# A 64-byte gap moves behind w_gate's even chunks: attention and SwiGLU in one kernel on Trainium2

## The chip, the cores and the metric

The kernel runs on one core of one Trainium2 chip (trn2). The metric is the device time of one execution in microseconds (us); for three runs of the kernel before it was 1176.67 us in the median, 1175.26 to 1177.6. The engines of the core are named as in the profile: PE is TensorE (matmuls), PEld its weight loads, DVE is VectorE, ACT is ScalarE, POOL is GpSimd, SP is SyncE, whose queue issues most of the transfers. SBUF is the memory on the chip that the engines read, 128 partitions; an address here is a byte offset in a partition. PSUM is the memory into which TensorE writes.

## The reference

Block-causal attention of 8 batches, 8 heads, 576 tokens and head size 64, and behind it a SwiGLU feed-forward over the 4608 tokens, all in float32:

```python
scores = scale * np.matmul(q, k.transpose(0, 1, 3, 2))
scores = np.where(mask, scores, -1000000000.0)   # blocks of 64
...
attn = np.exp(scores)
attn = attn / (np.sum(attn, axis=-1, keepdims=True) + 1e-09)
x = np.matmul(attn, v)                            # as [4608, 512]
...
g = x @ w_gate                                    # [512, 1536]
silu = g * (1.0 / (1.0 + np.exp(-g)))
val = x @ w_val                                   # [512, 1536]
return (silu * val @ w_out).astype(np.float32)    # [1536, 512]
```

## The kernel before, in words

The 4608 tokens are cut into 18 tiles of 256. For each tile the feed-forward goes through the 1536 columns of w_gate and w_val in 12 chunks of 128, two chunks (an even one and the odd one behind it) to a stage: six stages to a tile, 108 in all. To keep float32 accuracy with the faster float32r matmul, each operand is split into a high and a low part, and a product is three matmuls: high by high, high by low, low by high. They are the lines 1105, 1106 and 1107 of the function `up`. In them the weights are the stationary operand (`lhsT`, 128 by 128, loaded anew for each matmul), and the tokens, the tiles `xhl`, are the moving one (128 by 256).

A stage computes, in this order, the even chunk of w_gate (array g_even in the profile), its odd chunk (g_odd), and the even and the odd chunk of w_val (both in v_all). The contraction runs over 512 rows, four pieces of 128, so each chunk takes 4 x 3 = 12 matmuls: 12 with g_even, 12 with g_odd, 24 with v_all, 48 to a stage. Then VectorE and ScalarE make silu(g) times val and split it into high and low parts (tiles `hhl`), and the down stage multiplies these with chunks of w_out (tiles `wo`) in the lines 1197 to 1199. There `hhl` is the stationary operand and `wo` the moving one, 128 by 512; the result goes to the PSUM tiles po or at. The down stage of one pair of chunks stands behind the up stage of a later one, so that TensorE alternates between the two kinds.

The attention of later batches is put between these stages: scores in line 569 (line 442 for the first batches, 653 for one of them), products with v in line 782. A planner written in the kernel (`in_order`) sorts all steps of all engines by ranks and by costs that are constants in the code; it doesn't look at addresses. From the fifth tile on (FINE = 4) the steps of an up stage are mostly kept together in the order above. In the first four tiles they are cut into pieces of three matmuls, and pieces of several stages and of attention come in mixed orders. The first two tiles run while the attention of the first two batches is still being made.

The weights come into the chip once. A transfer brings a raw chunk into a `wo` tile, ScalarE casts its high part into its place (line 983) and VectorE subtracts to get the low part (line 986). Those places are the six tiles at the head of the list of constants, each with the index 0 for the high and 1 for the low part. For some chunks of w_out, places in these arrays that are not yet taken serve as a temporary store (`AWAY`, line 915), from which they are written to memory (line 1005) and read by a few early down stages.

The tiles of the list lie behind one another in SBUF in the order of the list. Ahead of the weights stand `ident` (512 bytes to a partition), `ones` (256) and two single columns, and g_odd begins 64 bytes past a multiple of 128. A g_odd or g_even tile has 4 x 768 x 4 = 12288 bytes, a v_all tile 24576, both multiples of 128; so g_odd and v_all begin 64 bytes past a multiple of 128. Behind v_all stands a tile of 16 float32 numbers, 64 bytes, that nothing reads or writes (line 205). Behind it g_even begins at a multiple of 128, and so do the tiles of `xhl`, `wo` and `hhl` that follow.

Of the kernel before, what the change touches and what calls it, by code (L numbers as in the profile page):

```python
# [8 lines left out]
F32R = mybir.dt.float32r  # L9
# [9 lines left out]
def kernel(  # L19
# [75 lines left out]
    const = ctx.enter_context(tc.tile_pool(name="const", bufs=1))  # L95
# [106 lines left out]
    half_w, whole_w = [P, NDC, DFF // 2], [P, NDC, DFF]  # L202
    g_odd = [const.tile(half_w, F32R, name=f"g_odd{x}") for x in range(2)]
    v_all = [const.tile(whole_w, F32R, name=f"v_all{x}") for x in range(2)]
    const.tile([P, 16], F32, name="gap")
    g_even = [const.tile(half_w, F32R, name=f"g_even{x}") for x in range(2)]

    def w_at(which, x, i):

# [1246 lines left out]
```

## Time and profile before

| | |
|---|---|
| median of 3 runs | 1176.67 us (1175.26 to 1177.6) |
| the profiled execution | 1178.6 us |
| its span, from the first to the last instruction | 1176.7 us |
| mean granted TensorE clock | 0.991 |
| busy: PE, DVE, ACT, POOL | 1149.6, 746.6, 625.0, 322.1 us |
| moved by DMA | 197.41 MB |

The profile is one execution, taken by the hardware profiler. A busy time adds up the time in which an engine had an instruction at work. Matmuls are pipelined: one lasts some 280 ns from its start to its end, but the next starts after some 115 ns. What a matmul costs a busy TensorE is therefore the interval from its start to the start of the next one, and that is read from the timeline, not from the mean length. The timeline gives a start in us, a length in us, the engine, the line of the kernel, the operation, what it writes and reads by the names of the tiles, and the shape. A matmul is listed at the start of its streaming; the load of its weights is a row of PEld.

The rows of groups give a line, an engine, an operation and a shape, how often it occurs, the busy us and the mean ns of one, and the idle time of the engine ahead of it.

### The profile page before, as it was taken

To read this page: it belongs to the slowest core of one execution; us is meant where nothing else is said; L and a number is where in the kernel's file an instruction comes from. 1 tells how busy PE (TensorE), PEld (TensorE's weight loads), DVE (VectorE), ACT (ScalarE), POOL (GpSimd) and SP (SyncE) were. 2 spreads that over 40 slices of the span, in tenths; PEclk is the share of its full clock that TensorE was granted. 3 is DMA by queue.
4 is the path that set the end of the run, shared out by engine and by line. 5 is a ranking of instruction groups with operands and counts; after the bars stand their busy time and mean duration, and the time that the engine had idled before them with its cause. 6 is when DMAs were issued, how large, how long until landed. Compare 5 with 4: busy or idle time off the path is not lost.

```text
span 1176.7 us, 21979 instructions
## 1 busy us (share of the span) xinstructions
PE 1149.6 (98%) x8578; PEld 1029.6 (88%) x8578; DVE 746.6 (63%) x1230; ACT 625.0 (53%) x1114; POOL 322.1 (27%) x139
## 2 busy tenths in 40 slices
PE   6889999999999999999999999999999999999998
PEld 5567878888899998989899998989989898999997
DVE  5798889677678574768567674856648565423222
ACT  5788877646383655637374564637355463212111
POOL 3212100144523333422414332342424233000000
PEclk8899999999999999999999999999999999999999
DMA  7666858756574646755376544745556434654442
GB/s 202 168 169 189 208 178 259 190 175 175 162 180 134 172 143 172 210 176 129 132 201 199 146 150 134 216 140 163 157 161 192 166 108 148 199 160 133 146 166 103
DMA packets 266984, 197.41 MB, mean 168 GB/s; under 512 B 195264, under 2 KB 231376, under 8 KB 266880
## 3 DMA queue, kind: packets, MB, share of 16 engines
q1 hardware_dynamic: 264304, 195.29, 56.8%
q8 instruction: 67, 1.10, 0.4%
q10 hardware_dynamic: 2576, 0.72, 0.3%
q14 instruction: 37, 0.30, 0.1%
HBM read 171.57 MB, written 24.38 MB: 167 GB/s over the span
## 4 chain that ended last, share of the span: by engine, by line
PE 90%; DVE 3%; ACT 3%; DMA 2%; issue 1%; SPq 0%; POOL 0%; ACTq 0%; POOLq 0%; DVEq 0%
PE gv L1105 17%; PE gv L1107 16%; PE gv L1106 16%; PE po L1197 8%; PE po L1198 7%; PE po L1199 7%; PE at L782 7%; PE at L569 5%; PE at L653 1%; PE at L1197 1%; PE at L442 1%; PE at L1198 1%; PE at L1199 1%; DVE mx L710 1%; DMA qk<-in_k_dram 1%
## 5 line engine op out<-in xcount | busy, mean ns | idle before, releaser
L714 POOL PARTITION_ALL_REDUCE mx<-mx x80 | 141.0, 1811 | 441.7 <-DVE mx L710 131.6
L833 POOL PARTITION_ALL_REDUCE mx<-mx x48 | 178.5, 3766 | 229.1 <-DVE mx L710 210.0
L1105 PE MATMUL gv<-xhl,v_all 128*128 128x256 f32 x864 | 241.0, 279 | 0.0
L1107 PE MATMUL gv<-xhl,v_all 128*128 128x256 f32 x864 | 239.2, 277 | 0.0
L1106 PE MATMUL gv<-xhl,v_all 128*128 128x256 f32 x864 | 239.0, 277 | 0.0
L1142 DVE SCALAR_TENSOR_TENSOR t<-t,gv 128x512 f32<-128x512 f32 x108 | 73.8, 684 | 146.6 <-ACT t L1139 146.0
L1105 PEld LDWEIGHTS gv<-xhl,v_all 128*128 128x128 f32 x864 | 162.1, 188 | 3.4 <-issue 2.1
L1106 PEld LDWEIGHTS gv<-xhl,v_all 128*128 128x128 f32 x864 | 162.3, 188 | 0.8
L1155 DVE TENSOR_TENSOR hhl<-t,hhl 128x512 fp32r<-128x512 f32 x108 | 91.4, 847 | 112.3 <-ACT hhl L1152 109.0
L1107 PEld LDWEIGHTS gv<-xhl,v_all 128*128 128x128 f32 x864 | 162.2, 188 | 0.1
L1152 ACT CAST hhl<-t 128x512 fp32r<-128x512 f32 x108 | 67.3, 623 | 156.2 <-PE po L1198 114.4
L1197 PE MATMUL po<-wo,hhl 128*128 128x512 f32 x372 | 148.3, 399 | 0.7 <-ACT ob L1224 0.7
L1198 PE MATMUL po<-wo,hhl 128*128 128x512 f32 x372 | 145.6, 391 | 0.0
L1199 PE MATMUL po<-wo,hhl 128*128 128x512 f32 x372 | 145.3, 390 | 0.0
L738 DVE TENSOR_TENSOR sc<-sc,mx 128x640 f32<-128x640 f32 (+6 forms) x168 | 123.4, 774 | 20.4 <-POOL mx L714 20.4
L1139 ACT ACTIVATE t<-gv 128x512 f32<-128x512 f32 x108 | 64.6, 598 | 119.6 <-PE gv L1107 116.9
L1105 PE MATMUL gv<-xhl,g_even 128*128 128x256 f32 x432 | 124.2, 288 | 0.2 <-DVE t L1142 0.2
L742 ACT ACTIVATE sc<-sc 128x1024 f32<-128x1024 f32 (+3 forms) x104 | 105.8, 1030 | 32.5 <-DVE sc L738 31.4
L1106 PE MATMUL gv<-xhl,g_even 128*128 128x256 f32 x432 | 122.5, 283 | 0.0
L1107 PE MATMUL gv<-xhl,g_even 128*128 128x256 f32 x432 | 122.3, 283 | 0.0
L1105 PE MATMUL gv<-xhl,g_odd 128*128 128x256 f32 x432 | 120.4, 279 | 0.0
L1107 PE MATMUL gv<-xhl,g_odd 128*128 128x256 f32 x432 | 119.5, 277 | 0.4 <-DVE g_odd L986 0.4
(175 smaller groups left out, 2398.8 us busy)
## 6 DMA issues: line engine op xcount, KB each, us to landing
wo<-wo_d SPq DMA_DIRECT2D x200, 512.0 KB
out_dram<-ob SPq DMA_DIRECT2D x35, 256.0 KB
v<-in_v_dram SPq DMA_DIRECT2D x64, 128.0 KB
xt<-x_d SPq DMA_DIRECT2D x64, 128.0 KB
rt<-r_d SPq DMA_DIRECT2D x128, 64.0 KB
qk<-in_q_dram SPq DMA_DIRECT2D x112, 72.0 KB
qk<-in_k_dram SPq DMA_DIRECT2D x104, 72.0 KB
x_d<-xu SPq DMA_DIRECT2D x24, 288.0 KB
```

What stands on the lines that cost most here:

```text
L714: nc.gpsimd.partition_all_reduce(m, m, channels=P, reduce_op=bass_isa.ReduceOp.max)
L738: nc.vector.tensor_tensor(piece(c), scores_of(c), m, ALU.subtract)
L742: nc.scalar.activation(x, x, AF.Exp)
L782: nc.tensor.matmul(ps[0][own(x), 1 - i if sums else i, q0 - s0 : s1 - s0], lhsT=ones if sums else vt[0][:, 2 * lane + c, own(x)], rhs=sc[0 ...
L833: nc.gpsimd.partition_all_reduce(m, m, channels=P, reduce_op=bass_isa.ReduceOp.add)
L1105: nc.tensor.matmul(o, lhsT=hi[:, d], rhs=xhi[:, 0:w], start=first, stop=False)
L1106: nc.tensor.matmul(o, lhsT=hi[:, d], rhs=xlo[:, 0:w], start=False, stop=False)
L1107: nc.tensor.matmul(o, lhsT=lo[:, d], rhs=xhi[:, 0:w], start=False, stop=last)
L1155: nc.vector.tensor_tensor(hh[1][:, 0:n], t[0][:, 0:n], hh[0][:, 0:n].bitcast(F32), ALU.subtract)
L1197: nc.tensor.matmul(po, lhsT=hi, rhs=whi, start=i + y == 0, stop=False)
L1198: nc.tensor.matmul(po, lhsT=hi, rhs=wlo, start=False, stop=False)
L1199: nc.tensor.matmul(po, lhsT=lo, rhs=whi, start=False, stop=i + y == NFC - 1)
```

## The change

The unused tile of 64 bytes moves in the list from ahead of the g_even tiles to behind them. The two g_even tiles begin 64 bytes lower, 64 bytes past a multiple of 128 as g_odd and v_all do. What stands behind the gap in the list keeps its place. No instruction and no order is touched.

```diff
     half_w, whole_w = [P, NDC, DFF // 2], [P, NDC, DFF]
     g_odd = [const.tile(half_w, F32R, name=f"g_odd{x}") for x in range(2)]
     v_all = [const.tile(whole_w, F32R, name=f"v_all{x}") for x in range(2)]
+    g_even = [const.tile(half_w, F32R, name=f"g_even{x}") for x in range(2)]
     const.tile([P, 16], F32, name="gap")
-    g_even = [const.tile(half_w, F32R, name=f"g_even{x}") for x in range(2)]
```

## The prediction

> **What bounds the kernel now.** I read four views of the profile in this order: the page, the busy time by stretches together with the waits of TensorE, the groups of instructions by form, and the timeline of TensorE.
>
> From the page, the busy row of TensorE and the shares of the chain that ended last:
>
> ```profile
> PE 1149.6 (98%) x8578; PEld 1029.6 (88%) x8578; DVE 746.6 (63%) x1230; ACT 625.0 (53%) x1114; POOL 322.1 (27%) x139
> ...
> PE 90%; DVE 3%; ACT 3%; DMA 2%; issue 1%; SPq 0%; POOL 0%; ACTq 0%; POOLq 0%; DVEq 0%
> ```
>
> From the busy time by stretches (start and end, length, then busy us of PE, PEld, DVE, ACT and POOL), one row; then everything that TensorE waited for from 300 us to the end:
>
> ```profile
> 400.00:600.00 200.00, 200.00 (x1492) 183.45 (x1491) 130.70 (x206) 108.88 (x194) 70.33 (x24) 1.00 0.56 162
> ```
>
> ```profile
> PE po L1197 <- ACT ob L1224: 0.3, 1, 0.3
> PE gv L1105 <- DVE t L1142: 0.2, 1, 0.2
> ```
>
> TensorE is never idle between 400 and 600 us, at a granted clock of 1.00, and from 300 us on it waits 0.5 us in all. So from there on the time is the sum of the intervals between starts of matmuls: a nanosecond more or less on each comes out at the end one for one. A busy time cannot show these intervals, because the matmuls are pipelined. Groups by form, from 300 us on (the middle one of the three matmuls of a triple; the last number before the bar is the mean ns of one):
>
> ```profile
> L1106 PE MATMUL gv<-xhl,v_all 128*128 128x256 f32 x712 | 196.7, 276 | 0.0
> L1106 PE MATMUL gv<-xhl,g_even 128*128 128x256 f32 x356 | 100.6, 283 | 0.0
> L1106 PE MATMUL gv<-xhl,g_odd 128*128 128x256 f32 x356 | 98.3, 276 | 0.0
> ```
>
> Three lines of 356 are 1068 matmuls with g_even, 12 to a stage: 89 stages of 12 g_even, 12 g_odd and 24 v_all matmuls lie behind 300 us. The g_even ones are 7 ns longer, with the same moving operands. What one costs shows in the timeline (start, length, engine, line). An ordinary stage, which follows a down stage (po<-wo,hhl) and ends in one:
>
> ```profile
> 698.73 0.28 PE L1105 MATMUL gv<-xhl,g_even 128*128 128x256 f32 x1
> ...
> 700.16 0.28 PE L1105 MATMUL gv<-xhl,g_odd 128*128 128x256 f32 x1
> ...
> 701.52 0.28 PE L1105 MATMUL gv<-xhl,v_all 128*128 128x256 f32 x1
> ...
> 704.24 0.40 PE L1197 MATMUL po<-wo,hhl 128*128 128x512 f32 x1
> ```
>
> g_even: 1.43 us for 12, 119.2 ns each. g_odd: 1.36 us for 12, 113.3 ns. v_all: 2.72 us for 24, 113.3 ns. The stage: 5.51 us. Read alone, this says that weights at a multiple of 128 cost 6 ns more, and that the change takes this off. But the weights that lie 64 bytes past do not always run at 113.3 ns. The early tiles, whose stages are split and come in other orders, show it. One stretch, again behind a down stage:
>
> ```profile
> 201.41 0.40 PE L1199 MATMUL at<-wo,hhl 128*128 128x512 f32 x1
> 201.64 0.28 PE L1105 MATMUL gv<-xhl,g_odd 128*128 128x256 f32 x1
> ...
> 203.05 0.28 PE L1105 MATMUL gv<-xhl,v_all 128*128 128x256 f32 x1
> ...
> 205.88 0.28 PE L1105 MATMUL gv<-xhl,g_even 128*128 128x256 f32 x1
> ...
> 207.31 0.28 PE L1105 MATMUL gv<-xhl,g_odd 128*128 128x256 f32 x1
> ...
> 208.67 0.28 PE L1105 MATMUL gv<-xhl,v_all 128*128 128x256 f32 x1
> ```
>
> Here g_odd comes first: 12 in 1.41 us, 117.5 ns. v_all behind it: 24 in 2.83 us, 117.9 ns. Then g_even, 119.2 ns; and behind g_even the next g_odd, 12 in 1.36 us, is at 113.3 ns. The same array runs at two rhythms, and what lies between is a passage through g_even. A late stage that was cut in two, so that v_all follows a down stage directly:
>
> ```profile
> 836.33 0.39 PE L1199 MATMUL po<-wo,hhl 128*128 128x512 f32 x1
> 836.55 0.28 PE L1105 MATMUL gv<-xhl,v_all 128*128 128x256 f32 x1
> ...
> 839.38 0.28 PE L1105 MATMUL gv<-xhl,g_even 128*128 128x256 f32 x1
> ```
>
> 24 in 2.83 us: 117.9 ns, to the last of them. I read this as a state, a phase between the reading of one matmul's weights and the streaming of another's operand. Weights 64 bytes past a multiple of 128 can hold either of two rhythms, 113.3 or 117.8 ns, and keep the one in which they were entered: 36 matmuls in a row in the stretch above. Coming from a down stage they enter the slow one. Coming from g_even, where the offset changes by 64 bytes in mid-stream, they enter the fast one. The passage from g_odd to v_all at 203.05, two arrays of the same offset, changed nothing.
>
> **The change part by part.** It adds and removes no instruction, no wait and no transfer. The gap keeps its size, so every tile listed behind it, the moving operands and hhl among them, stays where it was. The two g_even tiles move down by 64 bytes. Each effect:
>
> First, g_even's own matmuls. They then have the offset, and the inner layout, of g_odd, and come behind a down stage as g_odd did at 201.64. I take 117.5 ns for the first 12: 1.41 us against 1.43, so -0.02 us a stage.
>
> Second, what g_even does to its successors. With all weights at one offset there is no change of offset between the arrays, so I expect what happened at 203.05, which is nothing: g_odd and v_all stay at the rhythm in which the stage was entered. 36 matmuls at 117.9 ns are 4.24 us; now they take 1.36 + 2.72 = 4.08 us. That is +0.16 us a stage, and +0.14 us with the first effect. Bounds: at 113.3 ns throughout the stage would take 48 x 113.3 = 5.44 us, 0.07 less than now. That is the other end, and it decides the sign. I take the slow one, as the rows at 201.64 and 836.55 are the operation itself from the same predecessor.
>
> Third, stages that follow attention products, not a down stage. The profile has both kinds, v_all behind the products of line 569:
>
> ```profile
> 607.32 0.30 PE L1105 MATMUL gv<-xhl,v_all 128*128 128x256 f32 x1
> ...
> 610.16 0.29 PE L569 MATMUL at<-qk,parts 128*128 128x288 f32 x1
> ```
>
> ```profile
> 597.39 0.30 PE L1105 MATMUL gv<-xhl,v_all 128*128 128x256 f32 x1
> ...
> 598.77 0.28 PE L1105 MATMUL gv<-xhl,g_even 128*128 128x256 f32 x1
> ```
>
> 24 in 2.84 us (118.3 ns), but 12 in 1.38 us, 115 ns with the longer first one in it. Ahead of the first stood the full set of these products, as it does ahead of most such stages, ahead of the second only its latter part; so I count these stages as slow. If some fifteen of them were fast, each would be 5.65 - 5.44 = 0.21 us less, 3.2 us in all. That goes into the range.
>
> Fourth, the writers of g_even, ScalarE's casts as an example:
>
> ```profile
> L983 ACT CAST g_even<-wo 128x512 fp32r<-128x512 f32 x8 | 5.4, 677 | 2.1 <-PE po L1199 2.1
> L983 ACT CAST g_odd<-wo 128x512 fp32r<-128x512 f32 x8 | 5.3, 674 | 0.8 <-DVE wo L978 0.8
> ```
>
> Eight casts at either offset differ by 3 ns each: nothing, and in the early part where TensorE still waits.
>
> A rule speaks against any effect at all. The Trainium skill, "SBUF — State Buffer", section "Who interferes with whom", gives TensorE two independent read ports, one for the moving operand and one for the weights, and says that it never waits on anyone. By that rule no start address matters and the change is worth nothing. The trace disagrees: 119.2 against 113.3 ns in one stage with the same moving operands.
>
> **The sum.** 89 stages x 0.14 us = 12.5 us. Taken off: stretches that run slow today already, such as v_all at 607.32 and 836.55, gain nothing; six like these at 24 x 4.5 ns are 0.65 us. Ahead of 300 us lie the other 228 g_even matmuls, which gain about 1.6 ns each (0.4 us), and some stretches behind g_even that lose their fast rhythm, like that at 207.31; I put these at +0.5 us net, by the length of such stretches, and 0 if waits hide it. Together +12.3 us. The profiled execution took 1178.6 us (span 1176.7, the rest around it), 1.9 us above the median of the runs; it would become 1190.9, and the median 1176.67 + 12.3 = 1189.0 us. No cover is needed, as nothing is hidden: a TensorE without idle time passes it all on, and the other engines, at 63% and less, get longer to keep up.
>
> **The rivals.**
> Faster: the stage is entered at the fast rhythm. The place is the first three matmuls of g_even behind the last one of the down stage; if these start 113 ns apart, all 48 do. 89 x 0.07 = 6.2 us, with the stretches that are slow today (0.65 us) and the early part (228 x 6 ns = 1.4 us) some 8 us: 1168.5 us. For it: 597.39 shows such an entry, and 113.3 is what these weights do in most of today's stages. Against it: 201.64 and 836.55, both behind a down stage. 0.10.
>
> A small gain: what restores the fast rhythm is not the change of offset but something else in passing from g_even to g_odd. Then g_odd and v_all stay at 113.3, and g_even gets 1.6 ns less: 1296 x 1.6 = 2.1 us, 1174.6 us. Against it: from g_odd to v_all at 203.05 nothing was restored. 0.04.
>
> No change: the 119.2 ns belong to the first place behind a down stage, or the skill's rule of independent ports holds: 1176.7 us. Against it: at 205.88 g_even is at 119.2 ns in mid-stage, behind v_all. 0.05.
>
> **How the numbers follow.** The slow rhythm in all or nearly all stages has 0.81. Its own range: down to 1183 if the fifteen stages behind attention products are fast (-3.2), and paces and the scatter of runs (1175.26 to 1177.6) take another 2 to 3; up to 1192 if every pace is 0.4 ns higher (89 x 48 x 0.4 = 1.7) with the scatter. This holds 8 in 10, so the range is 1183 to 1192. A measurement of this kernel tells about 0.2% (2.4 us) from no change; the small gain lies just inside that. Faster 0.10, same 0.09, slower 0.81.
>
> **What would show it.** In the timeline of the changed kernel an ordinary stage takes 5.65 us from the first g_even to the next down stage: 1.41, 1.41 and 2.83 us for the three arrays. In the groups by form the slow rhythm is known by its mean; for the stretch behind 836.55 it is
>
> ```profile
> L1107 PE MATMUL gv<-xhl,v_all 128*128 128x256 f32 x8 | 2.2, 280 | 0.0
> ```
>
> so the means of all three arrays should come together near 280 ns: g_even below its 283, the others above their 276. TensorE still waits under 1 us behind 300 us, and down stages are as long as now. Wrong would be g_odd or v_all at 276 ns (the rhythm is not held, or is entered fast), or g_even still at 283 (it was never the offset).

## The result, and the profile after

The changed kernel took 1186.54 us (median of 6 runs, 1185.08 to 1188.94) against 1175.62 us (median of 6 runs, 1173.13 to 1177.6) for the kernel before on the same chips: a ratio of 1.0095, 95% interval 1.0080 to 1.0111, so slower by 9.4 to 13.0 us. Its profiled execution took 1187.47 us with a span of 1185.5 us, 8.8 us more than the 1176.7 of before; the rest of the difference of the medians lies in the scatter of the runs, as the profiled execution of before stood 3.0 us above its median and this one 0.9 us above its own.

From the page after the change, the busy row and the shares of the chain that ended last:

```profile
PE 1158.6 (98%) x8578; PEld 1040.1 (88%) x8578; DVE 746.9 (63%) x1230; ACT 624.6 (53%) x1114; POOL 321.7 (27%) x139
...
PE 88%; ACT 4%; DMA 3%; DVE 3%; issue 1%; SPq 1%; POOL 0%; POOLq 0%; DVEq 0%; ACTq 0%
```

The count of matmuls is the same, and the busy times of VectorE, ScalarE and GpSimd moved by 0.4 us at most. TensorE has 9.0 us more, its weight loads 10.5. The groups by form from 300 us on (the number before the bar is the mean ns of one matmul):

```profile
L1106 PE MATMUL gv<-xhl,v_all 128*128 128x256 f32 x712 | 198.6, 279 | 0.0
L1106 PE MATMUL gv<-xhl,g_odd 128*128 128x256 f32 x356 | 99.3, 279 | 0.0
L1106 PE MATMUL gv<-xhl,g_even 128*128 128x256 f32 x354 | 98.8, 279 | 0.0
```

The three arrays have come together at 279 ns: g_even from 283, g_odd and v_all from 276. The timeline of an ordinary stage:

```profile
1008.70 0.28 PE L1105 MATMUL gv<-xhl,g_even 128*128 128x256 f32 x1
...
1010.11 0.28 PE L1105 MATMUL gv<-xhl,g_odd 128*128 128x256 f32 x1
...
1011.52 0.28 PE L1105 MATMUL gv<-xhl,v_all 128*128 128x256 f32 x1
...
1014.35 0.40 PE L1197 MATMUL po<-wo,hhl 128*128 128x512 f32 x1
```

12 in 1.41 us, 12 in 1.41 us, 24 in 2.83 us: 117.5 to 117.9 ns each. In a stage the array that was moved got 0.02 us faster, and the two that were not touched lost 0.16 us. The stage takes 5.65 us in place of 5.51.

### The profile page after: what moved, and what is told of

Its sections match the earlier page's. It is cut to its first block, busy times and chain, and to the rows that moved or that the text cites. A ratio compares the mean times of both kernels' runs of the same rounds, so it can differ in the third digit from the quotient of the medians.

```text
span 1185.5 us, 21979 instructions
## 1 busy us (share of the span) xinstructions
PE 1158.6 (98%) x8578; PEld 1040.1 (88%) x8578; DVE 746.9 (63%) x1230; ACT 624.6 (53%) x1114; POOL 321.7 (27%) x139
## 4 chain that ended last, share of the span: by engine, by line
PE 88%; ACT 4%; DMA 3%; DVE 3%; issue 1%; SPq 1%; POOL 0%; POOLq 0%; DVEq 0%; ACTq 0%
PE gv L1105 16%; PE gv L1107 16%; PE gv L1106 16%; PE po L1197 8%; PE po L1199 7%; PE po L1198 7%; PE at L782 7%; PE at L569 5%; PE at L653 1%; DMA wo<-in_moe_w_out_dram 1%; ACT sc L742 1%; PE at L1197 1%; PE at L1199 1%; PE at L1198 1%; ACT sc L460 1%
## 5 line engine op out<-in xcount | busy, mean ns | idle before, releaser
L1105 PE MATMUL gv<-xhl,g_even 128*128 128x256 f32 x432 | 123.0, 285 | 0.2 <-DVE t L1142 0.2
L1105 PE MATMUL gv<-xhl,g_odd 128*128 128x256 f32 x432 | 121.5, 281 | 0.0
L1107 PE MATMUL gv<-xhl,g_odd 128*128 128x256 f32 x432 | 120.9, 280 | 0.4 <-DVE g_odd L986 0.4
L1107 PE MATMUL gv<-xhl,g_even 128*128 128x256 f32 x432 | 121.1, 280 | 0.0
L1106 PE MATMUL gv<-xhl,g_even 128*128 128x256 f32 x432 | 120.9, 280 | 0.0
```

The lines of the kernel that those rows point to most:

```text
L1105: nc.tensor.matmul(o, lhsT=hi[:, d], rhs=xhi[:, 0:w], start=first, stop=False)
L1106: nc.tensor.matmul(o, lhsT=hi[:, d], rhs=xlo[:, 0:w], start=False, stop=False)
L1107: nc.tensor.matmul(o, lhsT=lo[:, d], rhs=xhi[:, 0:w], start=False, stop=last)
```

## The experiments

All kernels are variants of the changed one, and the diffs below are against it. Up to the last of these sections, what differs is only where small unused tiles push the arrays. Offsets are given modulo 256 bytes from the third experiment on, where that turned out to matter: in the kernel before, g_odd and v_all are at 192 and g_even at 0; in the changed kernel all three are at 192; `xhl`, `wo` and `hhl` are at 0 in both. What stands behind a shifted array is kept at 0. Each ratio is to runs of the kernel before on the same chip, whose medians were 1175.38 to 1176.36 us.

### All weights at a multiple of 128

```diff
+    const.tile([P, 16], F32, name="gap")
     g_odd = [...]
     v_all = [...]
     g_even = [...]
-    const.tile([P, 16], F32, name="gap")
```

> The gap stands ahead of g_odd, so all three weight arrays begin at a multiple of 128, as hhl and the moving tiles do. Theory A (held rhythm: weights at a multiple of 128 have one rhythm, 119 to 120 ns; weights 64 bytes past have two, 113.3 and 117.8, and keep the one they were entered in until the offset changes): all three arrays at 119.4 ns; against the kernel before, 3888 matmuls of g_odd and v_all lose 119.4 - 114.0 = 5.4 ns, +21 us, 1197 us. Theory C (only a change of offset between arrays counts, the offset itself costs nothing): as in the changed kernel, 117.8 ns for all, 1186.5 us.

Measured: 1196.68 us (2 runs), 1.0178 of the kernel before (1.0156 to 1.0201). One group of its profile stands for all three arrays:

```profile
L1106 PE MATMUL gv<-xhl,v_all 128*128 128x256 f32 x696 | 196.9, 283 | 0.0
```

283 ns is the mean that only g_even had before; an ordinary stage took 5.75 us. The offset itself costs, as theory A has it, and theory C falls: neither kernel has a change of offset within the stage, and this one is 10 us slower than the changed one.

### The moving tiles shifted as well

```diff
+        if tag == "xhl":
+            const.tile([P, 16], F32, name="gap_xhl")
         for place in range(len(slots[tag])):
             tiles_of(tag, place, variant)
+        if tag == "xhl":
+            const.tile([P, 48], F32, name="gap_behind_xhl")
```

> The changed kernel with the moving tiles xhl also 64 bytes past a multiple of 128, so that weights and moving operand have the same offset again. If the rhythm depends on the offset of the weights relative to the moving operand: as with all at a multiple of 128, about 119.4 ns throughout, 5184 x 1.6 = 8 us over the changed kernel, 1195 us. If it depends on the offset of the weights alone: 117.8 ns as in the changed kernel, 1186.5 us.

Measured: 1196.12 us (2 runs), 1.0173 (1.0153 to 1.0194).

```profile
L1110 PE MATMUL gv<-xhl,v_all 128*128 128x256 f32 x696 | 197.5, 284 | 0.0
```

The weights lie exactly where the changed kernel has them, and yet they run like aligned ones; an ordinary stage took 5.75 us again. So what counts is the offset of the weights against that of the moving operand: where the two are the same modulo 128, a matmul costs about 120 ns.

### g_odd as the aligned array

```diff
+    const.tile([P, 16], F32, name="gap")
     g_odd = [...]
+    const.tile([P, 16], F32, name="gap2")
     v_all = [...]
     g_even = [...]
-    const.tile([P, 16], F32, name="gap")
+    const.tile([P, 48], F32, name="gap3")
```

> g_odd alone at a multiple of 128, g_even and v_all 64 bytes past. Theory A: g_even 117.8 ns (entered from a down stage), g_odd 119.4, v_all behind it restored to 113.3: a stage of 1.41 + 1.43 + 2.72 = 5.56 us against 5.65 in the changed kernel and 5.51 before; 89 x 0.05 = 4.5 us above the kernel before, 1180 us. Theory D (what restores is the array that comes first behind the down stage, not any passage through the other offset): v_all stays at 117.8, g_odd at 119.4, 1188.5 us.

Measured: 1191.68 us (2 runs), 1.0136 (1.0113 to 1.0158). In the timeline, from g_odd to the end of a stage (line 1199 is the down stage here):

```profile
1004.11 0.28 PE L1107 MATMUL gv<-xhl,g_odd 128*128 128x256 f32 x1
...
1005.55 0.28 PE L1107 MATMUL gv<-xhl,v_all 128*128 128x256 f32 x1
...
1008.38 0.40 PE L1199 MATMUL po<-wo,hhl 128*128 128x512 f32 x1
```

g_odd, aligned, took 1.44 us (120 ns), and v_all behind it 2.83 us: 117.9 ns, not restored. Theory A in the form in which it was stated, that any passage through the other offset restores the fast rhythm, falls. Theory D has the right pattern (and a time 3 us too low). But this layout differs from the kernel before in a second way: v_all lies at 64 modulo 256 here, where it was at 192. So two readings were open: the aligned array must stand first (theory F), or the step out of it must go 64 bytes back and not forward (theory S). The next two kernels cross them.

### The two readings crossed

First the same order, with v_all and g_even at 192 (the gap ahead of v_all is 48 numbers in place of 16, the one at the end 16 in place of 48):

> As e2_odd_at_128 (g_odd alone at a multiple of 128, second in the stage), but counted modulo 256: g_odd at 0, and g_even and v_all at 192 as all weights of the changed kernel are, where e2_odd_at_128 had them at 64. Theory S (the step out of the aligned array must go from 0 to 192, that is 64 bytes back, to restore the fast rhythm; a step from 0 to 64 does not): g_even 117.8, g_odd 119.8, v_all 113.3 ns; 5.56 us a stage, 1180 us. Theory F (the aligned array must stand first, right behind the down stage): v_all stays at 117.8 ns, as e2_odd_at_128, 1191 us.

Measured: 1179.71 us (6 runs), 1.0031 (1.0015 to 1.0047).

```profile
1011.92 0.28 PE L1107 MATMUL gv<-xhl,g_odd 128*128 128x256 f32 x1
...
1013.36 0.28 PE L1107 MATMUL gv<-xhl,v_all 128*128 128x256 f32 x1
...
1016.08 0.40 PE L1199 MATMUL po<-wo,hhl 128*128 128x512 f32 x1
```

v_all: 24 in 2.72 us, 113.3 ns. 128 bytes of difference in where v_all and g_even lie, and nothing else in the stage, are worth 12 us. Then the order of the kernel before, g_even aligned and first, with g_odd and v_all at 64:

```diff
+    const.tile([P, 32], F32, name="gap")
     g_odd = [...]
     v_all = [...]
+    const.tile([P, 48], F32, name="gap2")
     g_even = [...]
-    const.tile([P, 16], F32, name="gap")
```

> As the kernel before (g_even aligned and first in the stage), but g_odd and v_all at 64 modulo 256 in place of 192. Theory S: the step out of g_even goes from 0 to 64 and restores nothing; g_even 119.4, g_odd and v_all 117.8 ns, 5.67 us a stage, 1190 us. Theory F: as the kernel before, 1175.4 us.

Measured: 1189.41 us (2 runs), 1.0113 (1.0090 to 1.0135).

```profile
1010.19 0.28 PE L1106 MATMUL gv<-xhl,g_odd 128*128 128x256 f32 x1
...
1011.60 0.28 PE L1106 MATMUL gv<-xhl,v_all 128*128 128x256 f32 x1
...
1014.43 0.40 PE L1198 MATMUL po<-wo,hhl 128*128 128x512 f32 x1
```

g_odd 117.5 ns, v_all 117.9 ns behind an aligned g_even. Theory S gave both times within 1 us, theory F is wrong in both. In ordinary stages the fast rhythm is restored by a step from 0 to 192 modulo 256, not by one from 0 to 64.

As a rule that is still too simple. Offset 64 holds both rhythms too. In the early tiles of the kernel with only g_odd aligned (e2_odd_at_128; g_even and v_all at 64), the step from 0 to 64 is taken twice in one stretch, with different results:

```profile
200.31 0.28 PE L1107 MATMUL gv<-xhl,g_odd 128*128 128x256 f32 x1
...
201.74 0.28 PE L1107 MATMUL gv<-xhl,v_all 128*128 128x256 f32 x1
...
204.48 0.28 PE L1107 MATMUL gv<-xhl,g_even 128*128 128x256 f32 x1
...
205.84 0.28 PE L1107 MATMUL gv<-xhl,g_odd 128*128 128x256 f32 x1
...
207.28 0.28 PE L1107 MATMUL gv<-xhl,v_all 128*128 128x256 f32 x1
207.40 0.28 PE L1108 MATMUL gv<-xhl,v_all 128*128 128x256 f32 x1
```

Behind the first g_odd, v_all settles on 113.3 ns from its fourth matmul on, and g_even takes 12 in 1.36 us; behind the second, v_all starts every 118 ns. The two passages through g_odd take 1.43 and 1.44 us, but their inner rhythm differs: the last six intervals of the first are 121, 120, 124, 118, 117 and 120 ns, those of the second 120 five times and then 118. So the aligned matmuls have two rhythms as well, an even and an uneven one. The kernel before and the three layouts with one aligned array (e2_odd_at_128, e5_odd_at_0_rest_192, e7_even_at_0_rest_64) hold 379 passages of at least nine aligned matmuls into another offset. Seven of them have an uneven end, with an interval of 123 ns or more among the last six, and in all seven the rule is turned around: five steps from 0 to 192 lead to the slow rhythm, two from 0 to 64 to the fast one. Of the other 372, 371 follow the rule. What sets the aligned rhythm was not varied.

### A passage within each triple

The gap between the high and the low tile of g_even, the high one at 192 and the low one at 0:

> The changed kernel with the gap between the high and the low tile of g_even: high at 192 modulo 256, low at 0, so that every triple of g_even passes once through the aligned offset and steps back to 192. Theory S with one passage enough: the eight matmuls with high weights at 113.3, the four with low ones at 119.4 ns, g_odd and v_all at 113.3; 5.46 us a stage, 4 us under the kernel before, 1171 us. If one passage is not enough: all near 118 ns, as the changed kernel, 1187 us.

Measured: 1187.89 us (4 runs), 1.0103 (1.0085 to 1.0121).

```profile
L1108 PE MATMUL gv<-xhl,v_all 128*128 128x256 f32 x703 | 196.6, 280 | 0.0
```

No gain: in all but three of the 80 whole up stages behind 300 us v_all stays at the slow rhythm. One aligned matmul between two others does not restore it.

### hhl shifted

Two gaps around `hhl`, as around `xhl` above: ahead of it 16 numbers (offset 64, 48 behind it), and in a second kernel 48 (offset 192, 16 behind it):

> The changed kernel with hhl, the stationary operand of the down stage, 64 bytes past a multiple of 128; its moving operand wo stays. If the down stage follows the same rule as the up stage, its settled interval drops from 227 to about 220 ns: 1236 matmuls x 6.7 ns = 8.3 us less, 1178 us, if the up stages are still entered at 117.8 ns. If the way in decides the rhythm and the way in is now the fast one, another 48 x 4.5 ns x 89 stages = 19 us less: 1159 us. If the down stage is not bound by this offset: 1186.5 us.

> As e4_hhl_at_64, but hhl at 192 modulo 256 in place of 64. If the sign of the offset between stationary and moving operand counts (theory S carried over to the down stage): the settled interval of the down stage is 220 ns, 8 us under the changed kernel, 1178 us. If it does not: 233 ns as in e4_hhl_at_64, about 1192 us.

Measured: 1191.73 us (4 runs), 1.0139 (1.0119 to 1.0158), and 1184.33 us (2 runs), 1.0069 (1.0048 to 1.0091). Neither is near any of the times expected for it. The question of the second kernel is answered with yes: the sign counts. Twelve matmuls of the down stage (line 1201 here), first at 64, then at 192:

```profile
1007.66 0.39 PE L1201 MATMUL po<-wo,hhl 128*128 128x512 f32 x1
...
1010.45 0.28 PE L1109 MATMUL gv<-xhl,g_even 128*128 128x256 f32 x1
```

```profile
1009.59 0.40 PE L1201 MATMUL po<-wo,hhl 128*128 128x512 f32 x1
...
1012.35 0.28 PE L1109 MATMUL gv<-xhl,g_even 128*128 128x256 f32 x1
```

2.79 and 2.76 us, where the changed kernel takes 2.73 (below). For the down stage, with a moving operand of 512 columns in place of 256, the aligned offset is the best of the three. That the second kernel is still 2 us under the changed one comes mostly from up stages that run at the fast rhythm throughout, 5.44 us for 48 matmuls. Of the 80 whole up stages behind 300 us, 64 stand behind a down stage, 13 behind attention and 3 behind v_all of another up stage. With `hhl` at 192, 12 of the 64, 11 of the 13 and 1 of the 3 have that rhythm; in the changed kernel 0, 1 and 1. One of the 12:

```profile
698.14 0.28 PE L1109 MATMUL gv<-xhl,g_even 128*128 128x256 f32 x1
...
703.58 0.39 PE L1201 MATMUL po<-wo,hhl 128*128 128x512 f32 x1
```

48 in 5.44 us, entered from a down stage, with no aligned weights anywhere in the up stage. With `hhl` at 64 the same counts are 0, 12 and 0. So the way in is no fixed property of a down stage or of attention: the layout of `hhl`, which the up stage does not read, changes the rhythm in which the up stage is entered.

### Offsets of 32 bytes

All weights 32 bytes below and 32 bytes above a multiple of 128:

> All three weight arrays at 224 modulo 256 (32 bytes below a multiple of 128), with no change of offset in the stage. If the unit that counts is 64 bytes and only its parity: as one of the two known cases, 117.8 ns (1186.5 us) or 120 ns (1196.7 us). If the distance to the moving operand counts in smaller steps, a third rhythm; entered at 113.3 ns throughout it would be 5.44 us a stage, 7 us under the kernel before, 1169 us.

> All three weight arrays at 160 modulo 256 (32 bytes above a multiple of 128). Same question as e9_all_at_224 from the other side: 117.8 ns (1186.5 us) or 120 ns (1196.7 us) if only 64-byte parity counts; another rhythm, down to 113.3 ns (1169 us), if smaller distances count. If the sign counts as it did for the step out of the aligned array, this one is the slower of the two.

Measured: 1184.46 us (3 runs), 1.0076 (1.0048 to 1.0104), and 1198.29 us (2 runs), 1.0189 (1.0159 to 1.0219). Ordinary stages took 5.60 and 5.75 us, 116.7 and 120 ns a matmul. 224 gives a rhythm of its own, between the two known ones, held through the stage; 160 is as slow as aligned weights. So the side counts here too, though 160 is the mirror of 224 modulo 128 only, not modulo 256. Neither of the two is entered from a down stage at 113.3 ns.

### A version that beats both

If the step back to 192 is what is worth having, the aligned part need not be all of g_even. One tile of two rows takes its place: the first row, at 192, holds the contraction pieces 0 and 1 (high and low), the second, at 0, the pieces 2 and 3. From the fifth tile on the pieces of g_even are taken in the order 2, 3, 0, 1, so the sums are added in another order; the writers of g_even follow the layout.

```diff
-    g_even = [const.tile(half_w, F32R, name=f"g_even{x}") for x in range(2)]
-    const.tile([P, 16], F32, name="gap")
+    halves = const.tile([P, 2, 2 * DFF + 16], F32R, name="g_even")
+    g_even = [
+        halves[:, :, x * DFF : (x + 1) * DFF].rearrange("p a (b f) -> p a b f", b=2) for x in range(2)
+    ]
+    const.tile([P, 48], F32, name="gap")
...
-                for ds in [range(NDC)] if j >= FINE else [[d] for d in range(NDC)]:
+                order = (2, 3, 0, 1) if not which and not y else range(NDC)
+                for ds in [order] if j >= FINE else [[d] for d in range(NDC)]:
```

> Built on theory S, to beat both kernels. g_even is laid out in two halves: contraction pieces 0 and 1 at 192 modulo 256, pieces 2 and 3 at 0; from the fifth tile on its pieces are taken in the order 2, 3, 0, 1. So six matmuls pass through the aligned offset, entered from the down stage, and the step back to 192 lies within g_even. Theory S with six enough: 6 at about 119 and 6 at 113.3 ns for g_even, g_odd and v_all at 113.3 throughout; 5.48 us a stage against 5.51 before; 84 stages x 0.035 = 3 us under the kernel before, 0.25%, 1172.7 us. If six are too few to settle: 117.8 ns behind them, 1187 us.

The same with the order 2, 0, 1, 3:

> As e12_half_passage with the pieces of g_even taken in the order 2, 0, 1, 3: three matmuls at offset 0, six at 192, three at 0, then g_odd. If three entered from a down stage are enough: the six behind them at 113.3 ns, 5.48 us a stage and 1172.7 us as e12_half_passage. If three are too few at the head but the last three finish the work: the six at 117.8 ns, g_odd and v_all at 113.3, about 5.51 us, 1176 us. If neither is enough: 117.8 ns for g_odd and v_all, 1187 us.

Measured: 1174.35 us (11 runs, 1171.85 to 1175.25) against 1176.36 us (21 runs): 0.9982, interval 0.9973 to 0.9991, faster than the kernel before by 1.1 to 3.2 us and than the changed one by about 1%. The second: 1175.99 us (8 runs), 1.0002 (0.9991 to 1.0014). In the first one's timeline, the first aligned matmul, the first at 192 and the first of g_odd (line 1120 is the old 1105):

```profile
1007.88 0.28 PE L1120 MATMUL gv<-xhl,g_even 128*128 128x256 f32 x1
...
1008.59 0.28 PE L1120 MATMUL gv<-xhl,g_even 128*128 128x256 f32 x1
...
1009.27 0.28 PE L1120 MATMUL gv<-xhl,g_odd 128*128 128x256 f32 x1
```

Six in 0.71 us (118 ns), then six in 0.68 us (113.3 ns): the rhythm is restored within g_even. The stage takes 5.47 us in place of 5.51. The gain is 2 us where 3 were expected; the interval reaches both. Three of the 16 whole stages that do not stand behind a down stage took 5.66 us, not restored, which is some 0.5 us of it. In the second kernel, ordinary stages take 5.47 us too: behind a down stage three aligned matmuls are enough. Elsewhere they mostly are not: all 13 stages behind attention and two of the other three took 5.66 us or more, which gives the gain back.

## Why the prediction was right

**The mechanism.** Both rhythms, and the loss of the fast one in the two untouched arrays, came as forecast: 1.41, 1.41 and 2.83 us a stage, 279 ns for all three means, 1186.5 us in a range of 1183 to 1192. The faster rival was decided at the head of g_even: the fourth matmul starts 0.35 us after the first (1009.05 - 1008.70 in the timeline), 117 ns each, the slow rhythm. "No change" falls with g_even's 283 turned to 279. The small gain, another cause of the restoring that would leave g_odd and v_all at 113.3, falls with their 279.

**What was incomplete.** The prediction took any change of offset in mid-stage to restore the fast rhythm. That was enough for this change, which leaves none, but it is wrong as a rule: in ordinary stages a step from 0 to 64 restores nothing, one from 0 to 192 does. Had the change been the layout with g_odd and v_all at 64, the same reasoning would have missed 14 us. The trace before had a row against it even for 0 to 192, behind a g_even with the uneven rhythm:

```profile
342.77 0.28 PE L1105 MATMUL gv<-xhl,g_odd 128*128 128x256 f32 x1
...
344.18 0.28 PE L1105 MATMUL gv<-xhl,v_all 128*128 128x256 f32 x1
```

This g_odd takes 1.41 us, the slow rhythm. That a down stage leads into the slow rhythm was read from two stretches; it held for all 64 whole stages here, but with `hhl` at 192 it does not. The phase between the two reads, by which the prediction explains the state, is shown by no run.

**The sum** was +12.3 us; the medians differ by 10.9 us and the spans of the two profiled executions by 8.8. Four terms were off.

The stages: nine of the 89 are cut into parts, in which not every array ran fast before. The timelines hold 80 whole up stages behind 300 us, and 78 of them got slower; 78 x 0.14 = 10.9, less 0.15 for the other two, is near the 10.6 us by which the intervals of all up stages behind 308 us grew.

Stages behind attention were all taken as slow; 12 of the 13 whole ones were. This is the other one:

```profile
541.48 0.30 PE L1105 MATMUL gv<-xhl,g_even 128*128 128x256 f32 x1
...
546.95 0.30 PE L569 MATMUL at<-qk,parts 128*128 128x288 f32 x1
```

48 in 5.47 us. That only one of 13 was fast is in part luck: with `hhl` at 64 or 192 nearly all of them were, a case for which the prediction had 3.2 us in its range.

The down stages were forecast to be as long as before. Those behind an up stage got shorter: a down stage of twelve before and after the change, up to the next up stage,

```profile
704.24 0.40 PE L1197 MATMUL po<-wo,hhl 128*128 128x512 f32 x1
...
706.99 0.28 PE L1105 MATMUL gv<-xhl,g_even 128*128 128x256 f32 x1
```

```profile
1005.97 0.40 PE L1197 MATMUL po<-wo,hhl 128*128 128x512 f32 x1
...
1008.70 0.28 PE L1105 MATMUL gv<-xhl,g_even 128*128 128x256 f32 x1
```

2.75 and 2.73 us: 0.02 us in each of 46, 0.9 us in all; most of those behind attention took 2.77 us in both kernels. The state that an up stage leaves behind shapes the first matmuls of the next stage too.

And ahead of 300 us, put at +0.5 us, the changed kernel was the faster one: the same g_even matmul starts at 308.09 us before and at 307.43 us after the change.

```profile
308.09 0.28 PE L1105 MATMUL gv<-xhl,g_even 128*128 128x256 f32 x1
```

```profile
307.43 0.28 PE L1105 MATMUL gv<-xhl,g_even 128*128 128x256 f32 x1
```

That is not shown to be the gap's doing. The intervals of the up stages ahead of it grew by 0.75 us in all, near the forecast, and those of the down stages by 0.6; those of attention, with TensorE's waits in them, shrank by 2.0, and the longest wait went from 5.8 to 4.6 us. In the twelve experiments the same matmul starts at 304.6 to 307.5 us, whatever the layout. So the one profiled execution of before is the latest of fourteen here, and long early waits in it are the likelier cause; it also stood 3.0 us above its median. Together: +10.6 for the up stages behind 308 us, -0.9 for the down stages there, -0.1 for attention and -0.7 ahead of it make the 8.8 us between the spans, up to rounding.

**What stays open.** Why the rhythms exist is not shown, nor what sets the way in. The runs show that the interval depends on the offset of the weights against the moving operand, with its sign, and on the rhythm in which a matmul was entered; no counter of the profile shows what the reads of the two operands do in SBUF. Nor was a g_even with three aligned matmuls at the head and nine at 192 tried. By the two last kernels it should gain another 0.02 us in each stage behind a down stage and lose 0.17 us in each of the 13 behind attention, an estimate by which it is no better than the half passage.

## What to carry to other kernels

When TensorE has no idle time, read the intervals between the starts of its matmuls, array by array, and look for the same array at two intervals: then it is not the array's cost but a state, and an edit at one array is paid for or repaid at its neighbours. Where both operands come from SBUF, the start of each modulo 256 bytes is a tuning parameter, here of 2% between the best and the worst layout; try it for weights and moving operand together, and judge it by the whole stage. A slow operation that puts its successors in a better state can be worth keeping, and worth shortening to the part that does so.

## What the runs showed of the hardware

That a matmul of 128 by 128 by 256 in float32r has several lasting intervals at the same granted clock of 1.00 was in the first trace, but not how they depend on the layout: 120 ns with weights and moving operand at the same offset modulo 128, whether both are at 0 or one at 192 and the other at 64; 120 ns with the weights 32 bytes above; 116.7 ns with the weights 32 bytes below; 117.8 or 113.3 ns with the weights at 192, by the way in; 117.8 ns with the weights at 64 in ordinary stages, but 113.3 ns in stretches of the early tiles (v_all at 201.74 us in e2_odd_at_128). The way in depends on the layout of the stage ahead: with `hhl` at 192, 12 of 64 whole stages behind a down stage ran at 113.3 ns throughout, with `hhl` at 0 none. For 512 moving columns the order is another: aligned is best (2.73 us for twelve, behind an up stage in the slow rhythm), 192 next (2.76), 64 worst (2.79). The Trainium skill, "TensorE: Matmul & The Clock Gate", section "Step-by-step: what each phase is for", says that loading the next weights "doesn't steal SBUF read bandwidth from the running matmul". These runs do not show whether bandwidth is taken, but the interval is not independent of how the two operands lie to each other: with the same instructions and the same data, moving the moving operand alone by 64 bytes turned 117.8 ns into 120.
